# A finer load and cast of the second weight block, a two-step output, and a second product that may run late, in a fused retention and MLP kernel

## The chip, the cores and the metric

The kernel runs on one core of a Trainium2 chip. The metric is the device time of one execution in microseconds (us). The kernel before took 292.72 us (median of 3 runs, 292.54 to 293.72).

## The reference

A retention layer (attention without softmax, with a decay mask) over 8 batches, 8 heads, 576 positions and 64 dimensions, followed by an MLP with squared relu over the resulting 4608 tokens.

```python
scores = scale * q @ k.T                       # per batch and head
ret    = scores * Dmat                         # gamma_h ** (i - j) for i >= j, else 0
x      = (ret @ v).transpose(0, 2, 1, 3).reshape(4608, 512)
h      = x @ w_in                              # 512 x 2048
g      = np.maximum(h, 0) ** 2
out    = g @ w_out                             # 2048 x 512
```

## The kernel before

The tokens form 36 units of 128, two units to a group, 18 groups. For each group TensorE makes scores (`psc`), state sums (`psS`) and the output (`psO`) of the retention. VectorE masks the scores (`rx`), updates the state (`stmp`, `R`) and scales the output into `xT`. Then come the first product (`ph`, 64 matmuls with `w_in`), relu on ScalarE (`rl`), the square (`gT`) and the second product (`po`, with `w_out`). Groups 0 and 1 run their second product plainly, 16 matmuls of 512 columns a unit; later groups use Strassen's scheme. Groups 0 to 3 load two units of q, k or v at a time (`pair`).

All work is put down as tasks with a key (its priority), an assumed duration, dependencies and counted buffers. A small list scheduler in Python plays these tasks through once, at build time, and thereby fixes the order of every engine's instruction queue. Where TensorE has nothing to do in the scheduler's view, it places up to 40 junk matmuls (`warm`).

```python
WARM = 40
LAG = {"v2": 1.2, "w1": 1.3, "k4": 0.7, "q4": 0.5}     # corrections to the assumed landing times
sched = Schedule(dict(ff=4, prS=1, prO=1, ...))        # ff: PSUM buffers shared by psT, psS, ph, po
```

Each 1 MB weight block (0 to 3 of `w_in`, 4 to 7 of `w_out`) is one load and two casts:

```python
def add_weight(i):
    ...
    nc.sync.dma_start(out=t, in_=w_in[:, fb * 512:(fb + 1) * 512].rearrange("(m p) f -> p m f", p=P))
    ...
    t = dma_task(0, 2.75, fn, acq=("wst",), after=2.1 + LAG.get(f"w{i}", 0.0))
    for j, eng in enumerate(("POOL", "ACT")):          # GpSimd casts one half, ScalarE the other
        ...
        halves.append(add(eng, key, 1.05 if eng == "POOL" else 1.0, fc, deps=[t]))
```

The output of a paired group is one task, which needs the masked scores and the state:

```python
def fo():
    tile_of["psO", g] = ps_ret.tile([P, 2, 512], FP32, name="psO", tag="prO")
    inter(1)                    # matmuls on the state R
    nc.tensor.drain()
    ...                         # 32 matmuls on the masked scores rx
    inter(0)                    # matmuls on R again
t = add("PE", base + 24, 1.3, fo, deps=masked + [T["R", u]] + ([T["R", u - 1]] if carry else []), acq=("prO",))
```

The plain second product chains its units: each `po` task depends on the one before, over unit borders too.

```python
f2 = T["ff2"][-1:] if s == 0 else f2[-1:]
for fi in range(NF):
    ...
    f2.append(add("PE", base2 + NF * s + fi, 0.216, f, deps=[sq[fi // nf]] + wcast[4 + fi // 4] + f2[-1:],
                  acq=("ff",) if fi == 0 else ()))
```

Of the kernel before, what the change touches and what calls it, by code (L numbers as in the profile page):

```python
# [103 lines left out]
def kernel(  # L104
# [9 lines left out]
    nc = tc.nc  # L114
# [3 lines left out]
    P = 128  # L118
    NP = H // 2
    NF = DFF // P  # L120
# [169 lines left out]
    def add_load_pair(name, u):  # L290
# [3 lines left out]
        def fn():  # L294
            if name != "q":
# [3 lines left out]
        loaded[name, u] = loaded[name, u + 1] = dma_task(0, 1.81 if loaded else 2.9, fn, acq=("wst",) if name != "q" else (),  # L299
                                                         after=2.1 + LAG.get(name + str(u), 0.0))  # L300

    def add_weight(i):
        fb = i % 4

        def fn():
            if i < 4:
                t = stage.tile([P, NP, 512], FP32, name=f"wi{fb}", tag="wst")
                nc.sync.dma_start(out=t, in_=w_in[:, fb * 512:(fb + 1) * 512].rearrange("(m p) f -> p m f", p=P))
            else:
                t = stage.tile([P, 4, DM], FP32, name=f"wo{fb}", tag="wst")  # L310
                nc.sync.dma_start(out=t, in_=w_out[fb * 512:(fb + 1) * 512, :].rearrange("(n p) m -> p n m", p=P))
            tile_of["w", i] = t
        t = dma_task(0, 2.75, fn, acq=("wst",), after=2.1 + LAG.get(f"w{i}", 0.0))
        dst = w_in16[:, :, fb * 512:(fb + 1) * 512] if i < 4 else w_out16[:, fb * 4:(fb + 1) * 4, :]

        halves = []
        for j, eng in enumerate(("POOL", "ACT")):
            rows, sl = (slice(0, 4), slice(256 * j, 256 * j + 256)) if i == 0 else (slice(2 * j, 2 * j + 2), slice(0, 512))

            def fc(eng=eng, rows=rows, sl=sl):  # L320
                s = tile_of["w", i]
                (nc.gpsimd.tensor_copy if eng == "POOL" else nc.scalar.copy)(out=dst[:, rows, sl], in_=s[:, rows, sl])  # L322
            key = -50 + i if i or j == 0 else -17.5
            halves.append(add(eng, key, 1.05 if eng == "POOL" else 1.0, fc, deps=[t]))
        sched.free("wst", halves)
        wcast[i] = halves

# [9 lines left out]
    T = {}  # L337
# [8 lines left out]
    def half(x):  # L346
        return slice(64 * x, 64 * x + 64)
# [90 lines left out]
    def add_ret_pair(g):  # L438
# [40 lines left out]
        for s in range(2):  # L479
            src = None if s == 0 and not carry else u + s - 1  # L480

            def fr1(s=s, src=src):
                r = tile_of["tmp", u + s] = work.tile([P, NP * D], FP32, name="stmp", tag="stmp", bufs=1)
                nc.vector.tensor_tensor(out=r, in0=rT["sum"][s][:, 0:256], in1=tile_of["R", src], op=ALU.add)

            def fr2(s=s, src=src):
                r = tile_of["R", u + s] = st_pool.tile([P, NP * D], FP16, name="R", tag="R")
                x = rT["sum"][s][:, 0:256] if src is None else tile_of["tmp", u + s]
                nc.vector.tensor_tensor(
                    out=r.rearrange("p (n d) -> p n d", d=D), in0=x.rearrange("p (n d) -> p n d", d=D),  # L490
                    in1=dec128.rearrange("p (n o) -> p n o", o=1).to_broadcast([P, NP, D]), op=ALU.mult)
            if src is not None:
                chain.append(add("DVE", base + 5.5 + s, 0.42, fr1, deps=[t] + chain[-1:] + [T["R", src]]))
                T["Rread", src].append(chain[-1])
                sched.free("ff", chain[-1:])
            chain.append(add("DVE", base + 5.6 + s, 0.5, fr2, deps=[t] + chain[-1:], acq=("R",)))
            if src is None:
                sched.free("ff", chain[-1:])
            T["R", u + s], T["Rread", u + s] = chain[-1], []
# [12 lines left out]
                 start=(g, s, col) not in begun)  # L512
            begun.add((g, s, col))

        def fo():
            tile_of["psO", g] = ps_ret.tile([P, 2, 512], FP32, name="psO", tag="prO")
            inter(1)
            nc.tensor.drain()
            for m in range(NP):
                for e in range(2):  # L520
                    for s, b in ((0, 0), (1, 1), (0, 1), (1, 0)):
                        h = 2 * m + b
                        put2(s, h, tile_of["vx", u][half(s), e, 64 * h:64 * h + 64],
                             rT[e][half(s), m % 2, 2 * (m // 2) + b, :], s)
            inter(0)
        t = add("PE", base + 24, 1.3, fo, deps=masked + [T["R", u]] + ([T["R", u - 1]] if carry else []), acq=("prO",))
        for s in range(2):
            sched.free("kqT", [t])
            sched.free("kq", [t])
# [274 lines left out]

    def wcast_of(fi):
        w = wcast[fi // 4]
        return w[:1] if fi < 2 else w

    def add_ff(g):
        us = groups[g]  # L810
        n = len(us)
        base = min(us) * L

        def place(x):

            return base + x if g < last_g else base - NF * n - 1 + SPREAD * x
        nf = 4 // n
        f1 = []
        sq = []
        for fb in range(NF // nf):  # L820
            for j in range(nf):
                def f(fb=fb, j=j):
                    if j == 0:
                        tile_of["ph", g, fb] = ps_ff.tile([P, nf, n * P], FP32, name="ph", tag="ff")
                    fi = nf * fb + j
                    for m in range(NP):
                        nc.tensor.matmul(tile_of["ph", g, fb][:, j, :], lhsT=w_in16[:, m, fi * P:(fi + 1) * P],  # L827
                                         rhs=tile_of["x", g][:, m, :], start=(m == 0), stop=(m == NP - 1))
                f1.append(add("PE", place((nf * fb + j) * n), 0.01 + 0.2133 * n, f,
                              deps=[T["x", u] for u in us] + wcast_of(nf * fb + j) + f1[-1:],  # L830
                              acq=("ff",) if j == 0 else ()))

            def fr(fb=fb):
                t = tile_of["rl", g, fb] = r_pool.tile([P, nf, n * P], FP16, name="rl", tag="rl")
                nc.scalar.activation(out=t, in_=tile_of["ph", g, fb], func=ACTF.Relu)  # L835

            on_act = g >= STRASSEN and fb in (SQ_ACT if g < last_g - 1 else SQ_LATE)

            def fg(fb=fb, on_act=on_act):
                if fb == 0:  # L840
                    tile_of["g", g] = g_pool.tile([P, NF, n * P], FP16, name="gT", tag="gT")
                t = tile_of["g", g][:, nf * fb:nf * (fb + 1), :]
                rl = tile_of["rl", g, fb]
                if on_act:
                    nc.scalar.activation(out=t, in_=rl, func=ACTF.Square)  # L845
                else:
                    nc.vector.tensor_tensor(out=t, in0=rl, in1=rl, op=ALU.mult)  # L847
            r = add("ACT", place(4 * fb + 4), 0.6, fr, deps=[f1[-1]], acq=("rl",))
            sched.free("ff", [r])
            sq.append(add("ACT" if on_act else "DVE", place(4 * fb + 6), 0.63 if on_act else 0.55, fg, deps=[r] + sq[:1],  # L850
                          acq=() if fb else ("g",)))
            sched.free("rl", [sq[-1]])
        sched.free("x", [f1[-1]])
        base2 = base + NF * n
        if STRASSEN <= g:
            add_strassen(g, us, base2, sq)
            return
        for s, u in enumerate(us):
            end = base2 + NF * (s + 1)
            f2 = T["ff2"][-1:] if s == 0 else f2[-1:]  # L860
            for fi in range(NF):
                def f(fi=fi, s=s, u=u):
                    if fi == 0:
                        tile_of["po", u] = ps_ff.tile([P, DM], FP32, name="po", tag="ff")
                    nc.tensor.matmul(tile_of["po", u], lhsT=tile_of["g", g][:, fi, s * P:(s + 1) * P],  # L865
                                     rhs=w_out16[:, fi, :], start=(fi == 0), stop=(fi == NF - 1))
                f2.append(add("PE", base2 + NF * s + fi, 0.216, f, deps=[sq[fi // nf]] + wcast[4 + fi // 4] + f2[-1:],
                              acq=("ff",) if fi == 0 else ()))

            def fo(u=u):  # L870
                tile_of["o", u] = o_pool.tile([P, DM], FP32, name="o", tag="o")
                nc.scalar.copy(out=tile_of["o", u], in_=tile_of["po", u])
            oc = add("ACT", end + 1, 0.59, fo, deps=[f2[-1]], acq=("o",))
            sched.free("ff", [oc])
            st = add("SP", -0.5, 0.7, lambda u=u: store(u, tile_of["o", u]), deps=[oc], after=2.5, lag=LAG_O)
            sched.free("o", [st])
        sched.free("g", [f2[-1]])
        T["ff2"].append(f2[-1])

    def add_strassen(g, us, base, sq):  # L880
        n = len(us)
# [174 lines left out]
```

## Time and profile before

| | before |
|---|---|
| time, median of 3 | 292.72 us |
| span of the profiled run | 290.9 us |
| TensorE busy | 283.0 us (97%) |
| first `ph` matmul | 17.27 us |
| last junk matmul | ends at 21.06 us |
| `ph` on weight block 1 starts | 23.09 us |
| last cast of `w_out` starts | 37.10 us |

TensorE is busy nearly always, so its busy time says little. What says more is how much of its time is useful. I use a **lag**: the time since the start of the span, less the useful matmul work that TensorE has done by then. Work is counted from the trace, each matmul at the interval at which its kind follows itself: 109 ns for 256 columns, 217 ns for 512, 56 ns for `psT`, 9 to 19 ns for the small retention matmuls; junk counts nothing. All kernels do the same work, so at equal times the one with the smaller lag is ahead by the difference. The lag also grows a little in stretches full of small matmuls, in every kernel alike; only differences mean something. Each lag is read from one execution.

### The profile page before, as it was taken

What the parts mean: (1) busy time and instruction counts of PE and PEld (TensorE: products, weight loads), DVE (VectorE), ACT (ScalarE), POOL (GpSimd) and SP (SyncE); (2) the same over time, 40 slices, a digit from 0 to 9 for tenths busy, and PEclk for the clock granted to TensorE, in tenths of its full rate; (3) what the DMA queues carried; (4) which work ended last, traced back from release to release, by engine and by line L of the source; (5) the groups of instructions that cost most, each with busy time, mean ns of one, the idle gap of its engine ahead of it and who ended that gap; (6) DMA issues with size and microseconds to landing.
All of it is one profiled execution on the core that took longest, in us unless ns stands there. A gap on an engine that the chain in (4) does not pass through costs nothing.

```text
span 290.9 us, 10062 instructions
## 1 busy us (share of the span) xinstructions
PE 283.0 (97%) x4328; PEld 234.0 (80%) x4328; DVE 195.0 (67%) x430; ACT 187.5 (64%) x354; POOL 88.9 (31%) x123
## 2 busy tenths in 40 slices
PE   7989999999999999999999999999999999999994
PEld 2557765688888888888888888888888888888883
DVE  3796589748485848656868857667786865565632
ACT  6456966296757575867666666766767676747830
POOL 5343454524434234251616041615151400000000
PEclk9999999999999999999999999999999999999999
DMA  7999999999999899997998599979896820201004
GB/s 201 327 368 387 370 276 250 239 220 186 233 214 214 185 148 247 221 186 189 196 208 180 126 192 211 202 183 180 211 188 171 159 74 2 74 3 72 2 2 144
DMA packets 139421, 54.13 MB, mean 186 GB/s; under 512 B 118129, under 2 KB 130929, under 8 KB 139377
## 3 DMA queue, kind: packets, MB, share of 16 engines
q1 hardware_dynamic: 139072, 53.23, 81.9%
q8 instruction: 34, 0.56, 0.9%
q10 hardware_dynamic: 304, 0.26, 0.3%
q14 instruction: 11, 0.08, 0.1%
HBM read 36.70 MB, written 9.44 MB: 159 GB/s over the span
## 4 chain that ended last, share of the span: by engine, by line
PE 89%; DMA 6%; SPq 1%; issue 1%; POOL 1%; DVE 0%; DVEq 0%; POOLq 0%
PE ph L827 42%; PE po L916 34%; PE po L865 5%; PE psO L343 4%; DMA wi<-in_moe_w_in_dram 3%; DMA pair<-in_q_dram 3%; PE psc L343 2%; PE psS L343 2%; SPq L298 1%; POOL w_in L322 1%; PE psT L418 1%; DVE o L939 0%; POOL qx L403 0%; DVE p L968 0%; DVEq L939 0%
## 5 line engine op out<-in xcount | busy, mean ns | idle before, releaser
L827 PE MATMUL ph<-xT,w_in 128*128 128x256 f16 x1152 | 139.4, 273 | 0.2 <-POOL w_in L322 0.2
L827 PEld LDWEIGHTS <-w_in 128*128 128x128 f16 x1152 | 111.1, 98 | 14.8 <-POOL w_in L322 0.4
L835 ACT ACTIVATE rl<-ph 128x512 f16<-128x512 f32 x144 | 84.3, 589 | 46.9 <-PE ph L827 45.0
L845 ACT ACTIVATE gT<-rl 128x512 f16<-128x512 f16 x104 | 65.6, 631 | 3.0
L916 PEld LDWEIGHTS <-gS 128*128 128x128 f16 x512 | 49.4, 98 | 6.1 <-DVE gS L893 0.2
L916 PE MATMUL po<-wT,gS 128*128 128x256 f16 x384 | 52.4, 273 | 0.0
L893 DVE TENSOR_TENSOR gS<-gT,gS 128x512 f16<-128x512 f16 x64 | 35.1, 554 | 11.6 <-ACT gT L845 11.0
L916 PEld LDWEIGHTS <-gT 128*128 128x128 f16 x384 | 37.2, 98 | 4.4
L893 DVE TENSOR_TENSOR gS<-gT 128x512 f16<-128x512 f16 x64 | 30.7, 481 | 12.9 <-ACT gT L845 12.9
L916 PE MATMUL po<-w_out,gT 128*128 128x256 f16 x256 | 34.5, 273 | 0.0
L355 POOL CAST kq<-q 128x512 f16<-128x512 f32 x28 | 18.8, 673 | 45.7 <-DMA q<-in_q_dram 45.5
L367 POOL TENSOR_TENSOR v<-v,vdec_full 128x512 f16<-128x512 f32 x24 | 26.2, 1093 | 19.6 <-DMA v<-in_v_dram 14.4
L355 POOL CAST kq<-k 128x512 f16<-128x512 f32 x28 | 18.6, 666 | 44.4 <-DMA k<-in_k_dram 41.7
L847 DVE TENSOR_TENSOR gT<-rl 128x512 f16<-128x512 f16 x40 | 18.9, 473 | 14.7 <-ACT rl L835 14.2
L929 ACT COPY u<-po 128x256 f32<-128x256 f32 x32 | 11.8, 369 | 20.4 <-PE po L916 20.4
L939 DVE TENSOR_TENSOR o<-po,u 128x256 f32<-128x256 f32 x31 | 13.0, 421 | 16.2 <-PE po L916 8.3
L704 DVE TENSOR_TENSOR xT<-psO,gam_full 128x512 f16<-128x512 f32 x28 | 18.9, 686 | 7.5 <-PE psO L343 7.4
L643 DVE TENSOR_TENSOR rT<-psc,mask 128x512 f16<-128x512 f32 x28 | 18.3, 683 | 5.5 <-PE psc L343 5.2
L916 PE MATMUL po<-w_out,gS 128*128 128x256 f16 x128 | 17.0, 273 | 0.0
L916 PE MATMUL po<-wT,gT 128*128 128x256 f16 x128 | 16.8, 273 | 0.0
L939 DVE TENSOR_TENSOR o<-po,p 128x256 f32<-128x256 f32 x17 | 7.2, 424 | 13.7 <-ACT u L929 7.1
L865 PE MATMUL po<-w_out,gT 128*128 128x512 f16 x64 | 15.8, 380 | 0.0
(81 smaller groups left out, 244.1 us busy)
## 6 DMA issues: line engine op xcount, KB each, us to landing
out_dram<-o SPq DMA_DIRECT2D x31, 256.0 KB, 3.0
k<-in_k_dram SPq DMA_DIRECT2D x24, 256.0 KB, 4.5
q<-in_q_dram SPq DMA_DIRECT2D x24, 256.0 KB, 4.8
v<-in_v_dram SPq DMA_DIRECT2D x24, 256.0 KB, 5.3
wi<-in_moe_w_in_dram SPq DMA_DIRECT2D x4, 1024.0 KB, 10.1
wo<-in_moe_w_out_dram SPq DMA_DIRECT2D x4, 1024.0 KB, 9.7
pair<-in_k_dram SPq DMA_DIRECT2D x4, 512.0 KB, 7.0
pair<-in_q_dram SPq DMA_DIRECT2D x4, 512.0 KB, 7.0
```

The costliest lines, as they stand in the source:

```text
L343: nc.tensor.matmul(out_, lhsT=lhsT, rhs=rhs, start=start, stop=True, skip_group_check=True, tile_position=(64 * row, 64 * col))
L355: op(out=out_.rearrange("p (n b a d) -> p n b a d", n=2, b=2, a=2), in_=in_.rearrange("p (n a b) d -> p n b a d", n=2, a=2))
L367: nc.gpsimd.tensor_tensor(out=t, in0=tile_of["v32", u], in1=vdec[kind].rearrange("p (h o) -> p h o", o=1).to_broadcast([P, H, D]), op=ALU. ...
L704: nc.vector.tensor_tensor(out=tile_of["x", g][:, :, s * P:(s + 1) * P].rearrange("p n (c i) -> p c n i", c=2), in0=tile_of["psO", g][:, :, ...
L827: nc.tensor.matmul(tile_of["ph", g, fb][:, j, :], lhsT=w_in16[:, m, fi * P:(fi + 1) * P], rhs=tile_of["x", g][:, m, :], start=(m == 0), st ...
L835: nc.scalar.activation(out=t, in_=tile_of["ph", g, fb], func=ACTF.Relu)
L845: nc.scalar.activation(out=t, in_=rl, func=ACTF.Square)
L847: nc.vector.tensor_tensor(out=t, in0=rl, in1=rl, op=ALU.mult)
L865: nc.tensor.matmul(tile_of["po", u], lhsT=tile_of["g", g][:, fi, s * P:(s + 1) * P], rhs=w_out16[:, fi, :], start=(fi == 0), stop=(fi == N ...
L893: nc.vector.tensor_tensor(out=Sx(k, h), in0=in0(h), in1=in1(h), op=op)
L916: nc.tensor.matmul(tile_of["pb", g, bank], lhsT=left(i), rhs=right[:, i, :], start=(start and i == 0), stop=(i == HF - 1), skip_group_chec ...
L939: nc.vector.tensor_tensor(out=o_tile(u)[:, half * HM:(half + 1) * HM], in0=bank(x), in1=tile_of[name, g], op=ALU.add)
```

## The change

The intent is to let TensorE work in the opening, where it waits for weights. Weight block 1 comes in two loads, blocks 0 and 1 are cast in quarters. The output of a paired group is split so that the matmuls on the masked scores need not wait for the state. The second unit of group 0 gets a late key in its second product and no chain to the first, so that it fills gaps.

```diff
+    SPLIT = (1,)
+    NARROW = (0, 1)
...
-        t = dma_task(0, 2.75, fn, acq=("wst",), after=2.1 + LAG.get(f"w{i}", 0.0))
+        ts = [dma_task(0, 1.4 if i in SPLIT else 2.75, fn, acq=("wst",), after=2.1 + LAG.get(f"w{i}", 0.0))]
+        if i in SPLIT:
+            def fn2():
+                nc.sync.dma_start(out=tile_of["w", i][:, :, 256:512], ...)
+            ts.append(dma_task(0, 1.4, fn2, after=2.1 + LAG.get(f"w{i}", 0.0)))
...
+        for j, eng in enumerate(("POOL", "ACT", "POOL", "ACT") if narrow else ("POOL", "ACT")):
...
-            chain.append(add("DVE", base + 5.6 + s, 0.5, fr2, ...))
+            chain.append(add("DVE", base + (6.5 if u == 0 else 5.6) + s, 0.5, fr2, ...))
...
+        t = add("PE", base + 23.9, 0.6, fo1, deps=masked + T["kvx", u], acq=("prO",))      # matmuls on rx
+        t = add("PE", base + 24, 0.75, fo2, deps=[t, T["R", u]] + ...)                     # matmuls on R
...
-        return w[:1] if fi < 2 else w
+        return w[fi % 4:fi % 4 + 1] if fi // 4 in NARROW else w[:1] if fi < 2 else w
...
-            f2 = T["ff2"][-1:] if s == 0 else f2[-1:]
+            f2 = []
+            late = g == 0 and s == 1
...
-                f2.append(add("PE", base2 + NF * s + fi, 0.216, f, ...
+                f2.append(add("PE", 95.9 + fi / 1000 if late else base2 + NF * s + fi, 0.216, f, ...
```

More of the change, by code (lines that the diff above doesn't have):

```diff
@@ L307, in fn @@
                 t = stage.tile([P, NP, 512], FP32, name=f"wi{fb}", tag="wst")
-                nc.sync.dma_start(out=t, in_=w_in[:, fb * 512:(fb + 1) * 512].rearrange("(m p) f -> p m f", p=P))
+                lo = 256 if i in SPLIT else 512
+                nc.sync.dma_start(out=t[:, :, 0:lo], in_=w_in[:, fb * 512:fb * 512 + lo].rearrange("(m p) f -> p m f", p=P))
             else:
@@ L312, in fn @@
             tile_of["w", i] = t
-        t = dma_task(0, 2.75, fn, acq=("wst",), after=2.1 + LAG.get(f"w{i}", 0.0))
+        ts = [dma_task(0, 1.4 if i in SPLIT else 2.75, fn, acq=("wst",), after=2.1 + LAG.get(f"w{i}", 0.0))]
+        if i in SPLIT:
+            def fn2():
+                nc.sync.dma_start(out=tile_of["w", i][:, :, 256:512],
+                                  in_=w_in[:, i * 512 + 256:i * 512 + 512].rearrange("(m p) f -> p m f", p=P))
+            ts.append(dma_task(0, 1.4, fn2, after=2.1 + LAG.get(f"w{i}", 0.0)))
         dst = w_in16[:, :, fb * 512:(fb + 1) * 512] if i < 4 else w_out16[:, fb * 4:(fb + 1) * 4, :]
         halves = []
-        for j, eng in enumerate(("POOL", "ACT")):
-            rows, sl = (slice(0, 4), slice(256 * j, 256 * j + 256)) if i == 0 else (slice(2 * j, 2 * j + 2), slice(0, 512))
+        narrow = i in NARROW
+        for j, eng in enumerate(("POOL", "ACT", "POOL", "ACT") if narrow else ("POOL", "ACT")):
+            rows, sl = ((slice(0, 4), slice(128 * j, 128 * j + 128)) if narrow else
+                        (slice(0, 4), slice(256 * j, 256 * j + 256)) if i == 0 else (slice(2 * j, 2 * j + 2), slice(0, 512)))
             def fc(eng=eng, rows=rows, sl=sl):
@@ L322, in fc @@
                 (nc.gpsimd.tensor_copy if eng == "POOL" else nc.scalar.copy)(out=dst[:, rows, sl], in_=s[:, rows, sl])
-            key = -50 + i if i or j == 0 else -17.5
-            halves.append(add(eng, key, 1.05 if eng == "POOL" else 1.0, fc, deps=[t]))
+            key = -50 + i + 0.1 * j if i or j % 2 == 0 else -17.5
+            halves.append(add(eng, key, (1.05 if eng == "POOL" else 1.0) / (1.85 if narrow else 1), fc, deps=[ts[j // 2 if i in SPLIT else 0]]))
         sched.free("wst", halves)
@@ L495, in add_ret_pair @@
                 sched.free("ff", chain[-1:])
-            chain.append(add("DVE", base + 5.6 + s, 0.5, fr2, deps=[t] + chain[-1:], acq=("R",)))
+            chain.append(add("DVE", base + (6.5 if u == 0 else 5.6) + s, 0.5, fr2, deps=[t] + chain[-1:], acq=("R",)))
             if src is None:
@@ L513, in put2, with fo1 @@
             begun.add((g, s, col))
-        def fo():
+        def fo1():
             tile_of["psO", g] = ps_ret.tile([P, 2, 512], FP32, name="psO", tag="prO")
-            inter(1)
-            nc.tensor.drain()
             for m in range(NP):
@@ L524, in fo, with fo2 @@
                              rT[e][half(s), m % 2, 2 * (m // 2) + b, :], s)
+        def fo2():
             inter(0)
-        t = add("PE", base + 24, 1.3, fo, deps=masked + [T["R", u]] + ([T["R", u - 1]] if carry else []), acq=("prO",))
+            nc.tensor.drain()
+            inter(1)
+        t = add("PE", base + 23.9, 0.6, fo1, deps=masked + T["kvx", u], acq=("prO",))
+        t = add("PE", base + 24, 0.75, fo2, deps=[t, T["R", u]] + ([T["R", u - 1]] if carry else []))
         for s in range(2):
@@ L857, in add_ff @@
             return
+        ends = []
         for s, u in enumerate(us):
             end = base2 + NF * (s + 1)
-            f2 = T["ff2"][-1:] if s == 0 else f2[-1:]
+            f2 = []
+            late = g == 0 and s == 1
             for fi in range(NF):
@@ L866, in f @@
                                      rhs=w_out16[:, fi, :], start=(fi == 0), stop=(fi == NF - 1))
-                f2.append(add("PE", base2 + NF * s + fi, 0.216, f, deps=[sq[fi // nf]] + wcast[4 + fi // 4] + f2[-1:],
+                f2.append(add("PE", 95.9 + fi / 1000 if late else base2 + NF * s + fi, 0.216, f, deps=[sq[fi // nf]] + wcast[4 + fi // 4] + f2[-1:],
                               acq=("ff",) if fi == 0 else ()))
@@ L876, in add_ff @@
             sched.free("o", [st])
-        sched.free("g", [f2[-1]])
-        T["ff2"].append(f2[-1])
+            ends.append(f2[-1])
+        sched.free("g", ends)
+        T["ff2"] += ends
     def add_strassen(g, us, base, sq):
```

## The prediction

> **What bounds the kernel now.** I read the busy shares first, then the list of whom TensorE waited for, then TensorE's timeline over the opening, and last the timelines of the engines that feed it there. The page begins:
>
> ```profile
> PE 283.0 (97%) x4328; PEld 234.0 (80%) x4328; DVE 195.0 (67%) x430; ACT 187.5 (64%) x354; POOL 88.9 (31%) x123
> ```
>
> TensorE is busy 97% of a 290.9 us span. In the table of stretches it is busy 230.66 of the 231.12 us from 54.88 to 286.00. The change touches nothing there, so any gain must come from what TensorE does earlier. "Busy" also counts 40 matmuls on a junk tile (`warm`), which fill time in which nothing useful is ready. TensorE's timeline (start, duration, instruction, idle before it and who ended it) shows where they sit:
>
> ```profile
> 16.92 0.42 PE L343 MATMUL psc<-kqT 64*64 64x128 f16 x16
> 17.27 1.92 PE L827 MATMUL ph<-xT,w_in 128*128 128x256 f16 x16
> 19.03 0.59 PE L247 MATMUL warm<-junk 128*128 128x512 f16 x2
> 19.55 0.54 PE L343 MATMUL psS<-vx,kx 64*64 64x64 f16 x32
> 20.02 1.04 PE L247 MATMUL warm<-junk 128*128 128x512 f16 x4
> 22.00 0.31 PE L343 MATMUL psO<-kqT,R 64*64 64x128 f16 x8 [0.94 <-DVE R L489]
> 22.41 0.64 PE L343 MATMUL psO<-rx,vx 64*64 64x128 f16 x32
> 22.87 0.29 PE L343 MATMUL psO<-kqT,R 64*64 64x128 f16 x8
> 23.09 4.10 PE L827 MATMUL ph<-xT,w_in 128*128 128x256 f16 x36
> 27.35 3.23 PE L827 MATMUL ph<-xT,w_in 128*128 128x256 f16 x28 [0.15 <-POOL w_in L322]
> ```
>
> The reader is to see three things. The first product starts at 17.27 with 16 matmuls, which use up weight block 0. Between 19.03 and 22.00 only `psS` is useful. From 23.09 on there is no filler and one wait of 0.15 us. So the loss sits before 23.09; after that, all useful work is queued back to back. The two matters that hold the gap open are the arrival of weight block 1 and the state R that the second group's output needs. GpSimd's timeline gives the arrivals, because its casts wait for the landings:
>
> ```profile
> 18.03 1.04 POOL L399 TENSOR_TENSOR vx<-pair,vdec_pair 128x512 f16<-128x512 f32 x1 [1.93 <-DMA pair<-in_v_dram]
> 20.63 1.04 POOL L322 CAST w_in<-wi 128x1024 f16<-128x1024 f32 x1 [1.56 <-DMA wi<-in_moe_w_in_dram]
> 23.55 1.04 POOL L322 CAST w_in<-wi 128x1024 f16<-128x1024 f32 x1 [1.88 <-DMA wi<-in_moe_w_in_dram]
> 26.25 1.04 POOL L322 CAST w_in<-wi 128x1024 f16<-128x1024 f32 x1 [1.66 <-DMA wi<-in_moe_w_in_dram]
> ```
>
> Blocks 1, 2 and 3 land at about 20.6, 23.5 and 26.2, one per 2.7 to 2.9 us. The transfer rate in the table of stretches is 376 to 392 GB/s from 16 to 35 us, so the queue is full and block 2 cannot come sooner. VectorE's timeline in the same place:
>
> ```profile
> 20.48 0.41 DVE L484 TENSOR_TENSOR stmp<-psS,R 128x256 f32<-128x256 f32 x1
> 20.93 1.02 DVE L489 TENSOR_TENSOR R<-stmp,dec 128x256 f16<-128x256 f32 x1
> 22.05 0.43 DVE L484 TENSOR_TENSOR stmp<-psS,R 128x256 f32<-128x256 f32 x1
> 22.51 0.42 DVE L489 TENSOR_TENSOR R<-stmp,dec 128x256 f16<-128x256 f32 x1
> 23.23 1.36 DVE L537 TENSOR_TENSOR xT<-psO,gam_full 128x512 f16<-128x512 f32 x2
> ```
>
> The first R takes 1.02 us, the second 0.42. TensorE's wait of 0.94 us ends when the first is done, and `xT` of group 1 is ready only at 24.59.
>
> **What the Trainium skill says.** "SBUF — State Buffer", section "SBUF: two separate sides": VectorE instructions with two SBUF inputs and GpSimd instructions exclude each other for the whole instruction. The trace agrees: the 1.02 us R (inputs `stmp` and `dec`, both in SBUF) ends about 0.3 us after the GpSimd cast of 20.63 to 21.67 and is 0.6 us longer than its twin. "TensorE: Matmul & The Clock Gate", section "Wait — 56ns, not 53.3ns?": N columns at 2.4 GHz plus about 2.5 ns, so 109 ns for 256 columns and 216 ns for 512. The chain of waits agrees: 16 `ph` matmuls in 1.75 us, 4 `po` matmuls in 0.86. "DMA: Bandwidth & Descriptors", section "Measured (HBM→SBUF, 128 partitions, SWDGE, issued from GpSimd)": batch transfers to 1 MiB or more. That speaks against splitting; but it is given for another issuing path and for single transfers, and here the queue is never empty, so I take no loss. The kernel before has no 1 KB weight rows to check it on.
>
> **The change part by part.**
>
> *Block 1 by halves, cast in quarters (blocks 0 and 1).* Half of 1 MB at 388 GB/s is 1.35 us, so the first half lands at about 19.25 rather than 20.6. A quarter slice is half of 1.04 us plus some fixed cost; I estimate 0.57. Two engines take one slice each, so columns 0 to 255 of block 1 are ready at about 19.85 and the rest at 21.2, against 21.67 for the whole now. Block 0 (landed 15.03) gives its first slices at 15.6 instead of 16.1. Added: four cast instructions and one transfer issue of about 0.5 us on a queue that has time.
>
> *Output of a group in two steps.* The 32 `psO<-rx,vx` matmuls (0.64 us as shown) no longer wait for R: the masks are done at 20.2, so they fit before 21. Behind R remain 16 `psO<-kqT,R` matmuls and a drain, about 0.7 us, where now it is 1.1 (22.00 to 23.09). For the first group R moves behind the masks on VectorE, which lets the first step go earlier; `xT` of group 0 could come up to 0.8 us sooner (14.1 instead of 14.96).
>
> *What of this reaches the end.* The 16 block-1 matmuls of group 0 (1.75 us) now run from 23.09 to 24.84; afterwards they fit into the gap at 20 to 22.2. Starting block 0 earlier moves filler and gains nothing by itself, since after block 1 TensorE still has no work until either block 2 is cast (24.59) or group 1's `xT` is there. So the gain is 24.84 minus the earlier of those two. For `xT`: GpSimd's second slice of block 1 should end at 21.2, R then at 21.2 + 0.42 = 21.6 (now 21.95), remaining `psO` until 22.35, and the second R on VectorE until about 22.6, then two `xT` of 1.36 together: 23.95. From there group 1 has blocks 0 and 1 to work on. Gain: 24.84 - 23.95 = 0.9 us. The 0.15 us wait at 27.35 can go too. I take off 0.1 for new order and semaphores.
>
> *Second unit as filler.* From 24.84 to 38.45 TensorE is paced closely by the weight blocks: the last w_out cast starts at 37.10. In that stretch it does 111 matmuls busy 13.42 of 13.61 us. Arriving 0.9 us early, it would run out of first-product work 0.9 us before the last block. The second unit's product has 12 matmuls (blocks 0 to 2 of w_out, 12 x 0.216 = 2.6 us) that could run then and now don't. This part therefore earns nothing of its own; it keeps the 0.9 us from being lost again.
>
> Sum: 0.9 + 0.15 - 0.1, about 0.95 us off 292.72: 291.8.
>
> **The rivals.** (1) The gap only moves. The weight transfers set the pace up to 38 us, so an earlier TensorE waits at block 2, 3 or in the second product. For it: the 0.15 us wait at 27.35 exists already, and TensorE's backlog at 24.59 is only 0.25 us. Against: group 1's first product (64 matmuls, 7 us) needs only weights already there. If right, gain 0.2 to 0.3: 292.5. (2) PSUM or ScalarE takes over: the second unit holds one of the four `ff` buffers, and ScalarE is busy 11.50 of 13.61 us from 24.84 to 38.45 with casts and relus. Then some of the fill is paid for by first-product waits: 292.2 to 292.7. (3) More than I count: R undisturbed by GpSimd right behind `stmp`, or `xT` put before the second R, gives `xT` near 23.3 and a gain of 1.6: 291.1. (4) Later stages absorb it: group 2's inputs land at 40 to 42 and VectorE is busy 15.75 of 16.43 us from 38.45 to 54.88. Against: group 2's `xT` is done at 51.58, while `ph` restarts only at 54.88, and up to then TensorE is fed by second-product work; 3.3 us of slack is more than the gain.
>
> **Range and chances.** Most of it lies between rival 1 and rival 3: 290.7 to 292.8. A different emission order could cost a few tenths anywhere. Two per cent is 5.9 us; all filler and idle time between 19.03 and 23.09 is not 3 us, so faster by over 2% is nearly excluded, and a loss of that size would need a stall that nothing here suggests.
>
> **What would show it.** Right: `ph` on block 1 starts near 20 us; `psO<-rx,vx` comes before `psO<-kqT,R` and before R; `xT` of group 1 done at 23.5 to 24.2; no idle or filler over 0.3 us between 24 and 55; `po` of a second accumulator before 38; the instant where `ph` of group 2 restarts about 0.9 us before 54.88. Wrong: fillers or waits on `w_in`, `w_out` or ScalarE between 24 and 40; half transfers that land later than 19.6 and 21; block 2 later than 23.6; or a changed stretch after 55.

## More of the kernel before

With one core, runs differ by several tenths of a microsecond: one set of ten runs of the kernel before spans 292.65 to 293.67.

On the chip each engine works its queue in that order: an instruction that waits holds up all that stand behind it.

## The result, and the profile after

The changed kernel took 292.43 us (median of 4 runs, 292.40 to 292.56) beside 292.82 us for the kernel before (4 runs, 292.54 to 293.72). Ratios here are the mean time of one kernel's runs over that of the other's of the same rounds, so they are not quite the ratio of these medians. The ratio is 0.9982, with a 95% interval of 0.9960 to 1.0004. A second set gave 292.67 (6 runs, 292.18 to 293.64) beside 292.88 (10 runs), ratio 0.9996 (0.9975 to 1.0017). By medians that is 0.39 and 0.21 us gained; both intervals reach past 1, so a gain is not shown. Predicted was 292.72 - 291.8 = 0.92.

The page of the changed kernel shows the same busy time as before, but `ph` now waits 0.5 us for a cast of `w_in`, where it waited 0.2.

```profile
PE 283.0 (97%) x4328; PEld 233.7 (80%) x4328; DVE 195.8 (67%) x430; ACT 187.4 (64%) x356; POOL 87.8 (30%) x125
...
L842 PE MATMUL ph<-xT,w_in 128*128 128x256 f16 x1152 | 139.9, 273 | 0.5 <-POOL w_in L333 0.5
```

TensorE's timeline of the changed kernel in the opening (start, duration, instruction, idle time before it and who ended it):

```profile
16.79 0.64 PE L354 MATMUL psc<-kqT 64*64 64x128 f16 x32
17.36 1.48 PE L842 MATMUL ph<-xT,w_in 128*128 128x256 f16 x12
...
20.15 0.60 PE L247 MATMUL warm<-junk 128*128 128x512 f16 x2
20.59 0.60 PE L842 MATMUL ph<-xT,w_in 128*128 128x256 f16 x4
21.12 0.64 PE L354 MATMUL psO<-rx,vx 64*64 64x128 f16 x32
21.69 0.61 PE L842 MATMUL ph<-xT,w_in 128*128 128x256 f16 x4
22.23 0.71 PE L354 MATMUL psO<-kqT,R 64*64 64x128 f16 x16
22.87 1.05 PE L842 MATMUL ph<-xT,w_in 128*128 128x256 f16 x8
23.76 0.59 PE L247 MATMUL warm<-junk 128*128 128x512 f16 x2
24.88 6.29 PE L842 MATMUL ph<-xT,w_in 128*128 128x256 f16 x56 [0.52 <-POOL w_in L333]
```

The old gap is filled as intended: the 16 `ph` matmuls on block 1 run between 20.59 and 23.76, and `psO<-rx,vx` comes before `psO<-kqT,R`. But the filler and the wait have moved behind them. TensorE goes on at 24.88, when block 2 is cast. The kernel before had finished the same matmuls at 24.84 and went straight on. GpSimd's and VectorE's timelines of the changed kernel:

```profile
19.56 0.66 POOL L333 CAST w_in<-wi 128x512 f16<-128x512 f32 x1 [0.36 <-DMA wi<-in_moe_w_in_dram]
21.04 0.61 POOL L333 CAST w_in<-wi 128x512 f16<-128x512 f32 x1 [0.82 <-DMA wi<-in_moe_w_in_dram]
23.78 1.04 POOL L333 CAST w_in<-wi 128x1024 f16<-128x1024 f32 x1 [2.13 <-DMA wi<-in_moe_w_in_dram]
```

```profile
17.26 1.29 DVE L472 TENSOR_TENSOR rx<-psc,mask 128x512 f16<-128x512 f32 x2 [1.50 <-PE psc L354]
...
21.31 0.61 DVE L500 TENSOR_TENSOR R<-stmp,dec 128x256 f16<-128x256 f32 x1
...
23.16 1.35 DVE L552 TENSOR_TENSOR xT<-psO,gam_full 128x512 f16<-128x512 f32 x2
```

The two halves of block 1 are there at about 19.5 and 21.0, block 2 at 23.8. `xT` of group 1 is done at 24.51, almost as late as before (24.59). VectorE had stood idle for 1.50 us until 17.26, because the scores of group 1 (`psc`) now come at 16.79 in one piece, where the kernel before had them at 15.82 and 16.92. So `R` starts at 21.31, runs into GpSimd's second cast (21.04 to 21.65) and ends 0.27 us behind it, as in the kernel before (0.28).

The lag shows where the rest went. Lags of the two kernels at six instants (us; "again" is the second set's profile of the changed kernel):

| at | 24.8 | 31 | 41 | 50 | 60 | 285 |
|---|---|---|---|---|---|---|
| before | 16.20 | 16.52 | 16.70 | 16.94 | 17.74 | 23.99 |
| changed | 16.06 | 16.23 | 16.23 | 16.75 | 17.69 | 24.13 |
| changed, again | 16.06 | 16.16 | 16.14 | 16.83 | 17.61 | 23.92 |

Between 25 and 41 us the changed kernel wins about half a microsecond (0.47 and 0.56 at 41), and not where I had looked for it. By 60 us only 0.05 and 0.13 of it are left, and by 285 us nothing: the changed kernel is 0.14 behind in one trace and 0.07 ahead in the other. TensorE's last matmul starts at 286.83 in the kernel before, at 286.96 and 286.76 in the changed one. From there to the end of the span it takes 4.09 us before, 3.75 and 4.10 after, and 3.74 to 4.36 in all the traces told here. So this tail (the last sums, stores and semaphores) differs between two executions of one kernel by as much as the gain in question, and in the first pair of traces (spans of 290.9 and 290.7) it alone makes the changed kernel the shorter one. TensorE's timeline of the changed kernel at 48 us shows one place of the loss:

```profile
48.24 0.38 PE L882 MATMUL po<-w_out,gT 128*128 128x512 f16 x1
48.89 0.38 PE L882 MATMUL po<-w_out,gT 128*128 128x512 f16 x1 [0.26 <-DVE stmp L495]
49.19 0.64 PE L354 MATMUL psO<-rx,vx 64*64 64x128 f16 x32
```

A `po` matmul reads `w_out` and `gT`; `stmp` is none of its data. What `stmp` does is free one of the four `ff` buffers in PSUM, which held the state sums. The matmul at 48.89 is the first of a new unit and needs such a buffer. It stands in the queue in front of `psO` of group 2, so `psO` waits too. The kernel before had 4 `po` matmuls of an old unit at this place, and no wait.

### The profile page after: what moved, and what is told of

Its sections match the earlier page's. It is cut to its first block, busy times and chain, and to the rows that moved or that the text cites. A ratio compares the mean times of both kernels' runs of the same rounds, so it can differ in the third digit from the quotient of the medians. Undisturbed runs are those within 1.5% of the kernel's fastest.

```text
span 290.7 us, 10071 instructions
## 1 busy us (share of the span) xinstructions
PE 283.0 (97%) x4328; PEld 233.7 (80%) x4328; DVE 195.8 (67%) x430; ACT 187.4 (64%) x356; POOL 87.8 (30%) x125
## 4 chain that ended last, share of the span: by engine, by line
PE 89%; DMA 6%; SPq 1%; DVE 1%; POOL 1%; issue 1%; DVEq 0%
PE ph L842 43%; PE po L934 34%; PE po L882 4%; PE psO L354 4%; DMA wi<-in_moe_w_in_dram 4%; DMA pair<-in_q_dram 3%; PE psc L354 2%; PE psS L354 2%; SPq L298 1%; DVE rx L472 1%; POOL w_in L333 0%; PE psT L429 0%; DVE o L957 0%; POOL qx L414 0%; DVE p L986 0%
## 5 line engine op out<-in xcount | busy, mean ns | idle before, releaser
L911 DVE TENSOR_TENSOR gS<-gT,gS 128x512 f16<-128x512 f16 x64 | 34.4, 542 | 11.4 <-ACT gT L860 10.8
L911 DVE TENSOR_TENSOR gS<-gT 128x512 f16<-128x512 f16 x64 | 31.4, 492 | 12.9 <-ACT gT L860 12.8
L378 POOL TENSOR_TENSOR v<-v,vdec_full 128x512 f16<-128x512 f32 x24 | 25.4, 1059 | 20.3 <-DMA v<-in_v_dram 18.7
```

The costliest lines, as they stand in the source:

```text
L378: nc.gpsimd.tensor_tensor(out=t, in0=tile_of["v32", u], in1=vdec[kind].rearrange("p (h o) -> p h o", o=1).to_broadcast([P, H, D]), op=ALU. ...
L911: nc.vector.tensor_tensor(out=Sx(k, h), in0=in0(h), in1=in1(h), op=op)
```

## The experiments

Twelve kernels ran, in three sets of four. Each set shares its runs of the kernel before (medians 292.94, 292.88, 292.82); nine of the ten of the second set are those of the first. The lags of all, at the instants that matter:

| run | median us | ratio to before (95%) | 24.8 | 31 | 41 | 50 | 60 |
|---|---|---|---|---|---|---|---|
| e1_no_split | 292.40 | 0.9981 (0.9968 to 0.9994) | 16.05 | 16.33 | 16.40 | 16.65 | 17.44 |
| e2_one_step | 292.95 | 1.0002 (0.9988 to 1.0016) | 16.06 | 16.20 | 16.18 | 16.91 | 17.66 |
| e3_no_late | 292.73 | 0.9990 (0.9978 to 1.0003) | 15.93 | 15.92 | 16.61 | 16.90 | 17.68 |
| e4_r_first | 293.35 | 1.0010 (0.9997 to 1.0024) | 16.06 | 16.36 | 16.55 | 16.98 | 18.02 |
| f1_bank | 292.11 | 0.9971 (0.9957 to 0.9985) | 16.06 | 16.31 | 16.29 | 16.77 | 17.41 |
| f3_lag | 293.23 | 1.0011 (0.9996 to 1.0025) | 15.57 | 16.41 | 16.55 | 16.80 | 17.59 |
| f4_lag_no_split | 292.99 | 0.9999 (0.9987 to 1.0012) | 15.48 | 16.21 | 16.57 | 16.85 | 17.62 |
| h1_bank_lags | 293.35 | 1.0014 (0.9996 to 1.0033) | 15.79 | 15.83 | 15.81 | 16.80 | 18.58 |
| h2_state_lags | 292.96 | 1.0005 (0.9990 to 1.0020) | 16.00 | 16.00 | 15.97 | 16.60 | 18.40 |
| h3_state_lags_whole | 292.22 | 0.9981 (0.9967 to 0.9995) | 15.52 | 15.52 | 15.50 | 16.72 | 17.35 |
| h5_before_lags | 294.65 | 1.0055 (1.0042 to 1.0069) | 15.56 | 15.55 | 16.60 | 18.63 | 19.53 |

Theory A, formed after the result: the restart of the first product is set by block 2 and not by block 1 or the state, so that filling the old gap moves junk and no more; what the changed kernel gains it gains up to 41 us, and it loses it again at 48.9. The rivals are named in each expectation.

### e1_no_split: block 1 loaded whole

```diff
-    SPLIT = (1,)
+    SPLIT = ()
```

> The changed kernel with block 1 loaded whole again; quarter casts, two-step output and late second unit kept. Theory A (the first product after the gap is released by block 2, not by block 1 or the state, so filling the gap moves filler only): TensorE gets block 1 about 1.4 us later, but the matmuls on it now run without a gap into those on block 2; time within 0.2 us of the changed kernel (292.4), and blocks 2 and 3 land about 0.25 us earlier than in the changed kernel (23.55 and 26.25 against 23.78 and 26.48) if the half transfers slowed the stream. Theory B (early block 1 carries the gain): at least 0.5 us slower, 292.9 or more.

Measured: 292.40 us, in no way slower than the changed kernel's 292.43 and 292.67. So the half loads carry none of the gain in time; theory B falls. By its interval this kernel is even clear of the kernel before, as the changed one is not. Its lag is the same at 24.8, 0.1 to 0.2 us larger at 31, 0.2 to 0.3 larger at 41, and it has no wait at 48.9, so it is ahead at 60. The suspicion that half loads slow the stream falls too: from the start of GpSimd's `vx` on the state's values to the start of its cast of block 2 it takes 5.53 us here, 5.52 in the kernel before and 5.62 in the changed one, but with half loads also 5.53 in e2 and 5.52 in f3. What differed was the arrival of everything, already with `vx` (18.03, 18.07 and 18.16).

### e2_one_step: output in one step

```diff
-            chain.append(add("DVE", base + (6.5 if u == 0 else 5.6) + s, 0.5, fr2, ...))
+            chain.append(add("DVE", base + 5.6 + s, 0.5, fr2, ...))
-        t = add("PE", base + 23.9, 0.6, fo1, ...)
-        t = add("PE", base + 24, 0.75, fo2, ...)
+        t = add("PE", base + 24, 1.3, fo, ...)         # as before: inter(1), drain, rx, inter(0)
```

> The changed kernel with the paired output in one step again and the state's multiply at its old place; half loads, quarter casts and the late second unit kept. Theory A: block 2 still releases TensorE at about 24.8 us, so within 0.2 us of 292.4. Theory B (the two-step output carries what gain there is): 292.8, as before.

Measured: 292.95 us, as before, but with a lag within 0.16 us of the changed kernel's at each instant up to 60 (restart at 24.85, wait for `stmp` of 0.27). The clock says the two-step output is worth something, the lag says nothing of it is seen in the opening; between sets the changed kernel's own median moved by 0.24 us, so this run decides nothing.

### e3_no_late: no late second unit

```diff
-            f2 = []
-            late = g == 0 and s == 1
+            f2 = T["ff2"][-1:] if s == 0 else f2[-1:]
-                f2.append(add("PE", 95.9 + fi / 1000 if late else base2 + NF * s + fi, ...
+                f2.append(add("PE", base2 + NF * s + fi, ...
```

> The changed kernel without the late second unit (its second product is queued right behind the first unit's, as before). Theory A says that by 38 us the changed kernel is about 0.45 us ahead of the one before and loses most of it at 48.9 us, where a second-product matmul waits for a PSUM buffer that a VectorE add (stmp) frees: without the late unit no such wait, and a time of 292.0 (0.4 under the changed kernel). Rival C (the loss is just a later arrival of the data of group 2, or DVE): wait of the same size elsewhere between 41 and 57, time 292.4. Rival D (the late unit is needed as filler, as predicted): gaps before 38 us and 292.7 or more.

Measured: 292.73 us. The wait at 48.9 is gone, as theory A had it, but another one is there instead, as rival D had it. TensorE's timeline of this run:

```profile
38.36 3.18 PE L880 MATMUL po<-w_out,gT 128*128 128x512 f16 x14 [0.55 <-POOL w_out L333]
```

Without the late unit TensorE runs out of work and waits 0.55 us for the last block of `w_out`; the changed kernel had three more `po` matmuls in one run of 17 there (3 x 0.217 = 0.65 us). The lag grows by 0.69 from 31 to 41 us, in the changed kernel not at all. From 41 to 60 it grows by 1.07, in the changed kernel by 1.46 and 1.47. So the late unit saves about 0.7 us by 41, and the order that comes with it costs about 0.4 after that. That the lags at 60 are equal all the same is because the loads came earlier in this trace (block 2 at 23.47, against 23.78) and it was 0.31 ahead at 31. My figure of 292.0 was a miss.

### e4_r_first: the state ahead of the masks

```diff
-            chain.append(add("DVE", base + (6.5 if u == 0 else 5.6) + s, 0.5, fr2, ...))
+            chain.append(add("DVE", base + 5.6 + s, 0.5, fr2, ...))
```

> The changed kernel with the first group's state multiply ahead of the masks again (key 5.6). The score matmuls of group 1 should start near 15.9 instead of 16.8 us, so that the state of group 1 is ready near 21.5 and its xT near 24.0 (24.51 in the changed kernel). Theory A: TensorE still goes on with block 2 at 24.8, so 292.4 within 0.2. If xT of group 1 is what holds TensorE: 0.5 faster, 291.9.

Measured: 293.35 us, by medians the wrong way by 0.4 against before, though the interval (0.9997 to 1.0024) holds 1. `psc` did start earlier (15.80) and R was ready at 21.35, but eight `ph` matmuls stood in front of `psO` on R, which came at 22.23 as in the changed kernel; `xT` was done at 24.37. TensorE went on with block 2 at 25.00, because block 2 came at 23.90. That the restart hangs on block 2 holds; the size of the loss is not explained by it. Its lag is 0.33 to 0.41 us above the changed kernel's at 60 us.

### g0_after_again: the changed kernel beside the next three

> The changed kernel itself, unedited, beside the following three on one chip. 0.3 to 0.5 us under the kernel before.

Measured: 292.67 us (292.18 to 293.64), 0.21 under before, so a little less than expected. The wait of 0.3 us for `stmp` is there again.

### f1_bank: no buffer asked for in front of `psO`

```diff
+            if g == 1 and s == 1:
+                sched.need(f2[0], T["fo1", 2])      # first po of group 1's second unit after psO of group 2
```

> The changed kernel, where the first second-product matmul of group 1's second unit may only be queued after the first output step of group 2. Theory E: the changed kernel's opening gain of about 0.45 us at 38 us is given back at 48.9 us, where that matmul stands in front of psO in TensorE's queue and waits for a PSUM buffer that stmp frees; with the order changed no such wait and 0.3 to 0.45 us under the changed kernel. Rival F: psO itself could not start sooner, since its masks come from VectorE, which is the bound there: same time as the changed kernel within 0.15 us.

Measured: 292.11 us, 0.56 under the changed kernel of the same set by medians, and clear of the kernel before (ratio 0.9971, interval below 1). The list of waits has no `po` on `stmp` any more, and `psO` of group 2 starts at 48.62 instead of 49.19:

```profile
48.31 0.38 PE L882 MATMUL po<-w_out,gT 128*128 128x512 f16 x1
48.62 0.64 PE L354 MATMUL psO<-rx,vx 64*64 64x128 f16 x32
```

Rival F falls: VectorE's masks did not hold `psO`. The lag grows by 1.12 from 41 to 60 us, against 1.46 and 1.47, so the wait and what hung on it were worth 0.35 us there; at 60 it is 0.20 to 0.28 under the changed kernel's. By the clock this kernel beats both. Its trace does not show all of that in TensorE's work: the last matmul starts at 286.73, 0.03 to 0.23 us before that of the changed kernel and 0.10 before that of the kernel before, and its tail is a short one (3.74).

### f3_lag: the state's output step in front of block 1, and group 1 in front of block 2

```diff
 (f1_bank and e4_r_first, and)
+            if g == 0 and fb == 2:
+                sched.need(f1[nf * fb], T["fo2", 1])     # first ph on block 1 after psO on R of group 1
-    LAG = {"v2": 1.2, "w1": 1.3, ...
+    LAG = {"v2": 1.2, "w1": 1.3, "w2": 1.0, ...
```

> As f1, and besides: the state multiply ahead of the masks, block 1's first matmul queued behind the state's output step of group 1, and the scheduler told that block 2 comes 1.0 us later, so that 8 matmuls of group 1 on block 0 are queued before group 0's on block 2. Theory E says that the arrival of group 1's xT sets the restart once it is allowed to: psO of group 1 done near 22.1, xT near 23.5, no gap between 22 and 31, TensorE restarts on group 1 at about 23.9 instead of 24.88; 0.7 us or more under f1's expectation, 291.2 to 291.5. Rival G (transfers set the pace to 38 us, so an earlier restart is lost to waits on w_in block 3 or on w_out blocks): within 0.2 of f1.

Measured: 293.23 us. In the opening theory E is right: `psO` of group 1 ends about 22.5, its `xT` is done at 23.95, and TensorE does not stop at block 2. Its timeline:

```profile
22.46 4.54 PE L842 MATMUL ph<-xT,w_in 128*128 128x256 f16 x40
27.51 2.79 PE L842 MATMUL ph<-xT,w_in 128*128 128x256 f16 x24 [0.51 <-POOL w_in L333]
```

It is 0.49 us ahead of the changed kernel at 24.8, and behind it at 31. It waits 0.51 us for block 3 with ready matmuls of group 1 queued behind. Rival G holds for this order. From 60 us to 285 it lost another 0.8 us against f1 (its lag grows by 7.25, f1's by 6.48). The order of instructions is not the cause: after 60 us all engines of the two kernels work through the same sequence of tiles but for one matmul. The profiled execution was f3's slowest (293.57), so part may be scatter of one execution; the cause is not known.

### f4_lag_no_split: f3 with block 1 whole

```diff
-    SPLIT = (1,)
+    SPLIT = ()
```

> f3 with block 1 loaded whole. Since block 1 is cast at about 21.8 us and its first matmul is queued behind the state's output step that ends near 22.1, the split should be worth nothing here: within 0.15 us of f3. If the half transfers do carry the gain: 0.3 us or more slower than f3.

Measured: 292.99 us, 0.24 below f3, beyond the 0.15 that I had allowed but on the side that speaks against the half loads.

### h1, h2, h3: the scheduler told when the blocks come

The scheduler's own plan of f3, printed at build time, has the cast of block 3 at 25.1 us. The trace has it at 26.4. For block 2 the plan has 23.35 with the correction of 1.0, so 22.35 without, and the traces have 23.5 to 23.9. The six later blocks are all assumed 1.15 to 1.4 us too early (against f3's trace), so TensorE's queue is filled with work that is not ready yet. These kernels correct that.

```diff
-    LAG = {"v2": 1.2, "w1": 1.3, ...
+    LAG = {"v2": 1.2, "w1": 1.3, **{f"w{i}": 1.2 for i in range(2, 8)}, ...
 h1: with f1_bank.   h2: with f1_bank, e4_r_first and the need of f3_lag.   h3: h2 with SPLIT = ().
```

> f1, with the scheduler told that blocks 2 to 7 arrive 1.2 us later than it assumes (it assumes about 22.4 and 25.1 us for blocks 2 and 3; the chip shows about 23.6 and 26.4). The restart of TensorE stays at block 2 (24.6 to 25.0), since 16 matmuls of the changed order need it except 4 of group 1 in front. Expected within 0.2 us of f1 (292.1); if the order after the restart matters by itself, 0.3 or more off in either direction.

> f3 with the same later arrivals. In f3 TensorE ran without a gap from 22.46, was 0.5 us ahead of the changed kernel at 24.8 and lost it at 27.5 waiting for block 3 (0.51 us), behind which 24 ready matmuls of group 1 stood. Theory E': the wait was the queue order, not a lack of work; with 12 more of them queued in front of block 3 no wait at 27.5, 0.4 us or more under f1 at 60 us, time 291.6 to 291.9. Rival G: the transfers set the pace up to 38 us whatever the order; it waits at w_out blocks 0 to 3 instead and is within 0.2 of f1.

> h2 with block 1 loaded whole. f4 against f3 showed no loss from loading it whole (292.99 against 293.23). Expected within 0.2 us of h2: then the half loads are not needed for any of the gain.

Measured: h1 293.35, h2 292.96, h3 292.22 us. Up to 41 us all three are gapless and the furthest ahead: h3 has a lag of 15.50 there, 1.20 less than the kernel before. TensorE's timeline of h3 runs through, with 72 matmuls on `w_in` in a row:

```profile
22.31 8.15 PE L842 MATMUL ph<-xT,w_in 128*128 128x256 f16 x72
```

So rival G falls as far as 41 us: the wait for block 3 was the queue's order. But at 60 us h3 is only 0.39 ahead of before, and h1 and h2 are 0.84 and 0.66 behind. What they meet is groups 2 and 3. VectorE's timeline of h3:

```profile
42.42 0.69 DVE L410 TENSOR_TENSOR vx<-pair,vdec_pair 128x512 f16<-128x512 f32 x1 [2.27 <-DMA pair<-in_v_dram]
```

The values of group 2 land at 42.1 to 42.5 us in each kernel whose VectorE I looked at here (before 42.09, changed 42.48, f1 42.41, h1 42.40, h3 42.42, h5 42.46). In the kernel before VectorE waited 0.20 us for them, in h3 2.27, in h1 2.08. An opening that is finished earlier only waits longer there. In h1 TensorE then waits 0.87 us at 53.90 for a `vx` of group 3, in h2 0.58 at 52.73 for an `xT`. My 292.1 for h1 and 291.6 to 291.9 for h2 were misses by 1 us (for h1 the other branch came true: the order matters by itself); that of h3 against h2 was a miss as well, since h3 was 0.74 faster. In each of the three pairs (e1, f4 and h3) the kernel with block 1 whole was no slower than the one with half loads.

### h5_before_lags: the kernel before with the same corrected arrivals

```diff
-    LAG = {"v2": 1.2, "w1": 1.3, ...
+    LAG = {"v2": 1.2, "w1": 1.3, **{f"w{i}": 1.2 for i in range(2, 8)}, ...
```

> The kernel before with nothing changed but the later assumed arrivals of blocks 2 to 7. If the gain of the variants lies in the order alone: the wait of 0.3 us at 27.3 is gone and the time 0.3 us under before. If the change's parts are needed: within 0.15 us of before, 292.9.

Measured: 294.65 us, slower by 1.8. Yet from 22.39 to 34 us it is gapless with a lag of 15.55, nearly the best of all, with none of the parts of the change in it. GpSimd's and TensorE's timelines of this run:

```profile
20.87 1.27 POOL L322 CAST w_in<-wi 128x1024 f16<-128x1024 f32 x1 [1.06 <-DMA wi<-in_moe_w_in_dram]
21.30 0.31 PE L343 MATMUL psO<-kqT,R 64*64 64x128 f16 x8
22.39 8.10 PE L827 MATMUL ph<-xT,w_in 128*128 128x256 f16 x72
```

Most of that lead is not the edit's. The queues of TensorE and VectorE are those of the kernel before through the matmuls on block 1, and yet these begin at 22.39 instead of 23.09, and the lag at 24.8 is 0.64 smaller. Here `R` started at 20.82, before GpSimd's cast, and took 0.42 us; in the kernel before the cast was first (20.63), and `R`, started at 20.93, took 1.02. So `psO` on `R` came at 21.30 instead of 22.00. The cast waits for the load of block 1, so a few tenths of a microsecond in its arrival changed which of the two went first. The edit's own part is the vanished wait for block 3: the lag does not grow from 24.8 to 31, and in the kernel before it grows by 0.32. Then, without the late unit, TensorE waits 0.91 us for the last block of `w_out` and 0.99 us for a `vx` of group 2. So an order alone removes the waits on `w_in` in the opening, and the time is then decided by what follows.

## Why the prediction was right or wrong

The class (within 2%) and the range (290.7 to 292.8) held, but the range ended 0.08 us above the time of the kernel before, so that it also held no gain at all. The size did not hold: 0.92 us were predicted, 0.39 and 0.21 were measured, neither clear of zero. What gain the traces show up to 41 us came from other terms than the one that the prediction rested on; that the time lies in the range is luck as far as the mechanism goes. By its steps:

- **Where the loss sits.** Right. TensorE's filler lay before 23.09 us, the change moved it, and no other stretch holds junk.
- **Half loads, "ready at about 19.85 and the rest at 21.2, against 21.67 for the whole now".** Half right. The first slices were ready at 20.2 and the second at 21.65, so the second half came no sooner than the whole did. From `vx` to the casts it took 1.40 and 2.88 us, where the whole block took 2.60. e1, with the whole load, lost no time.
- **Output in two steps, `xT` at 23.95.** Wrong by 0.56 (24.51). R was ready at 21.92 instead of 21.6: group 1's scores came later (16.79), so R started at 21.31 and ran into GpSimd's second cast, which itself ended at 21.65 and not at 21.2. In e4, where R started at 20.93, it took 0.42 and was ready at 21.35. Then `psO` on R stood behind four `ph` matmuls, and a `gT` went in front of `xT`. The early start of group 0, which I had counted as free, was paid with group 1's scores.
- **"So the gain is 24.84 minus the earlier of those two", 0.9 us.** This is the step that failed. With `xT` at 24.51 even this sum leaves only 0.33. And queue order decides, not whichever comes first: the next matmuls in the queue were group 0's on block 2, and they started at 24.88. The gain of this term was about 0 (lags of 16.20 and 16.23 at 27 us). f3, where group 1 stands in front, restarts without a gap, so the lever that I named exists; this change does not pull it.
- **"The 0.15 us wait at 27.35 can go too."** Right, and under-counted: the lag of the kernel before grows by 0.32 there, that of the changed kernel by 0. The idle time in the list starts at the shown end of the last matmul, and a matmul is shown as 0.27 us long where the next could have started after 0.11.
- **Second unit as filler, "earns nothing of its own".** Under-counted. The kernel before loses 0.20 us at 38 already, where the prediction had all work after 23.09 queued back to back, and e3 loses 0.69 from 31 to 41 without the late unit. With the two terms above, that makes the 0.5 us that the changed kernel is ahead at 41.
- **Rival 1, "The gap only moves", 292.5.** This is what happened, in place and size: TensorE waited at block 2 (cast from 23.78, later than the 23.6 named as a sign of being wrong). Its reason, that the transfers set the pace up to 38 us, does not hold: h2 has the same loads (block 2 at 23.76) and no wait up to 41 us.
- **Rival 2, a PSUM buffer.** Named, but sought at 24.84 to 38.45 with ScalarE as its releaser. It came at 48.9, released by VectorE, and f1 shows that it can be ordered away.
- **Rival 4, "3.3 us of slack is more than the gain".** Wrong. I had read the slack from when `ph` of group 2 restarts. What matters is everything queued between 41 and 57 us: `psT`, `psc`, `psS` and `psO` of groups 2 and 3 wait on loads and on VectorE one by one. h3 loses 0.8 of its 1.2 us there, h1 and h2 all of theirs.

What stays open: whether the changed kernel gains anything at all; how much the two-step output is worth by itself (e2 was 0.28 and 0.52 us above the changed kernel's two medians, which differ by 0.24 themselves); whether e4 is really slower than before; and the differences of up to 1 us in lag that grow between 60 and 285 us (7.25 in f3, 6.25 in the kernel before), though the order of instructions there is nearly the same. What makes the tail long or short was not asked.

## What to carry to other kernels

Where a scheduler fixes each queue at build time, filling a gap earns only what the next instruction in the queue allows: look for what it waits for, and for ready work that stands behind it. Compare the useful work done by given instants, not idle time, since junk and waits trade places. Once the opening was gapless here, the next stage's loads and VectorE set the pace. A wait that names an engine whose data the instruction doesn't read may be a wait for a buffer. And before a gain of a few tenths is explained, see how much two traces of one kernel differ: here the tail after the last matmul differed by 0.35 us.

## What the Trainium skill lacked or had wrong

- "DMA: Bandwidth & Descriptors", section "Measured (HBM→SBUF, 128 partitions, SWDGE, issued from GpSimd)", advises transfers of 1 MiB or more and has no figure for a load split within a full queue. Here, by the starts of the casts, two halves of 0.5 MB landed 1.40 and 2.88 us after the load before them and the whole 2.60 us after it; the block behind them came after 5.62 us against 5.52, no loss beyond the scatter.
- "Perfetto Trace Analysis", section "Optimization Strategy", ties PSUM that ran out to consistent bubbles. The one here was a single wait of 0.26 us, filed under the VectorE instruction that freed the buffer (`stmp`), and ordering it away was worth 0.35 us of lag between 41 and 60 us.
